# The sixth expert's rows gathered in quarters of 128 columns and turned by VectorE

## The chip, the core and the metric

The kernel runs on one core of one Trainium2 chip. The metric is the device time of one execution, in microseconds (us); the median of three runs of the kernel before is 612.68 us (611.35 to 615.02). The core has TensorE (PE, with its weight loads as PEld), VectorE (DVE), ScalarE (ACT), GpSimd (POOL) and SyncE (SP), each with its own queue of instructions that it takes in order, and 16 DMA engines that move data between the chip's main memory and the on-chip buffer. The matmuls' sums go to a third memory, PSUM.

## The reference

A retention layer of 8 batches, 8 heads, 576 positions and 64 columns makes 4608 rows of 512 numbers, and a mixture of 8 experts works on these rows:

```python
def _moe_ref(x, w_gate, w1, w2):
    N, D = x.shape                       # 4608, 512
    E = w_gate.shape[1]                  # 8
    cap = N // E                         # 576
    flat = (x @ w_gate).flatten()
    order = np.argsort(-flat)
    ...                                  # best pairs first: a token goes to one expert, 576 tokens each
    for e in range(E):
        mask = assigned == e
        h = np.maximum(x[mask] @ w1[e], 0.0)   # 576 x 512 by 512 x 1024
        out[mask] = h @ w2[e]                  # 576 x 1024 by 1024 x 512
```

## The kernel before, in words

The retention layer and the first part of the routing fill the first 160 us. The rows x are then in main memory as `xd`, and also seen as `xq`, in which each row is four quarters of 128 columns. The experts follow one after the other, in an order that the router finds while they run. Experts are counted from 0 here, so the sixth expert is expert 5.

For an expert, `l1` (L1081) computes the first layer in 16 blocks: 8 pieces of 128 hidden columns, each for rows 0 to 255 and for rows 256 to 575. A block is 12 matmuls: four pieces of the 512 columns times three products, since every number is split into a high and a low part (`xh`, `xl`; `w1h`, `w1l`). `l2` (L1132) computes the second layer in five tiles: four of 128 rows, each in 8 steps of three matmuls with 512 columns, and one of 64 rows in 8 short steps of two.

Between these stand the things that the change touches:

- `gather` (L1016) brings the 576 rows of the next expert with POOL's indirect DMAs. For an expert under `PIECES` these are five DMAs of up to 128 whole rows. For the others they are 18 DMAs of 128 rows and 128 columns each, issued one by one as the planner's clock passes 1300 ns for each; their indices are made by `listing` (L505 to L510).
- `transposes` (L1046) puts the rows' columns on the partitions. For an expert under `PIECES` TensorE does it: 20 transposes in five groups of four into PSUM (`pt`, L1074), from which ScalarE copies `xh` and VectorE subtracts to make `xl`. For the others VectorE does it in blocks of 32 by 32 (`xz`, two buffers, L1058), ScalarE copies (L1060) and VectorE subtracts (L1061), and the columns come out in another order, which the second layout of the first-layer weights (`in_w1n`) has too.
- `conv` (L987) splits the weights. Where it is ScalarE and an accumulating POOL load that make the low part, the load is issued by L1009; for experts 6 and 7 it is VectorE (L1002).
- `l2` starts `transposes` of the next expert when the planner's clock `mix.t` is past `state['arrives']`, which `gather` has set 6000 or 9000 ns after its last DMA, and then takes one of its five parts with each step of the second layer.
- The router for the expert after the next runs at the same time. It is a chain: VectorE makes a table `G` (L191), TensorE counts with nine small matmuls (`r`, L383), and VectorE works out the next digit from the counts (L387 to L378). Seven of these chains make a search, followed by the members and the list of the expert (L451, L489). The `Mixer` decides after which matmuls a part of it is put down: it keeps two estimated clocks, `mix.t` for TensorE and `mix.v` for VectorE, and `mix.vec(ns)` adds to the second what a piece of VectorE's work should take.

So the order on each engine is fixed when the program is built, by these estimates, and at run time an engine takes its own queue in order. The lines on which the steps of the change rest are these:

```python
if e + 1 in XG and e + 1 not in XH and mix.t > state['arrives']:
    tr = transposes(e + 1)
next(tr, None)
...
if i == 0 and e >= PIECES:
    for _ in tr:
        pass
```

The second piece, in `l1`, puts down whatever part of the turning is left ahead of the first block.

Of the kernel before, what the change touches and what calls it, by code (L numbers as in the profile page):

```python
# [19 lines left out]
NP, HP, NB = 4, 4, 9  # L20
N, DM, E, FF = 4608, 512, 8, 1024
SLACK = 1.0
PIECES = 6

def consts_np():
    h = np.arange(H); g = (1.0 - 2.0 ** (-5.0 - h)).astype(np.float64)
# [61 lines left out]
class Route:  # L88
# [369 lines left out]
    def listing(s, p):  # L458
# [43 lines left out]
        if early:  # L502
            s.room(cn)
        if p >= PIECES:
            s.quarter = pool.tile([128, 20], I32, name="quarter", bufs=2)  # L505
# [439 lines left out]
def moe(tc, nc, P, R, xd, w1_d, w2_d, out, mix):  # L945
# [12 lines left out]
    def phases():  # L958
        for p in range(E):
# [9 lines left out]
            found.append(R.idx)  # L969
            if p >= PIECES:  # L970
                quarters[p] = R.quarter
# [5 lines left out]
    def dma_pump():  # L977

        while state['dma'] < min(state['conv'] + 4, 8*E):
            e, k = divmod(state['dma'], 8)  # L980
            if e not in regs or state['dma'] >= state['most']:
                return
            t = P['raw']()
            src = ((w1_d[0] if e < PIECES else w1_d[1]) if k < 4 else w2_d)
            nc.sync.dma_start(t, src[bass.ds(regs[e], 1), :, (k % 4)*1024:(k % 4)*1024+1024].rearrange("a p x -> (a p) x"))
            RAW[e, k] = t
            state['dma'] += 1  # L987

    def conv(fast=False):

        e, k = divmod(state['conv'], 8)
        if state['dma'] <= state['conv']:
            mix.drain(lambda: e in regs)
            dma_pump()
        raw = RAW.pop((e, k))
        nm = "w1" if k < 4 else "w2"
        hi = P['w'].tile([128, 1024], F32R, name=nm + "h", bufs=4)
        lo = P['w'].tile([128, 1024], F32R, name=nm + "l", bufs=4)
        A.activation(hi, raw, AF.Copy)
        if e >= PIECES:  # L1000
            for x in (slice(0, 512), slice(512, 1024)):
                V.tensor_tensor(lo[:, x], raw[:, x], hi[:, x].bitcast(F32), op=ALU.subtract)  # L1002
                mix.vec(690)
        elif fast:
            for x in (slice(0, 512), slice(512, 1024)):
                lows.append(lambda x=x: V.tensor_tensor(lo[:, x], raw[:, x], hi[:, x].bitcast(F32), op=ALU.subtract))
        else:
            A.activation(lo, raw, AF.Copy, scale=-1.0)  # L1008
            add = lambda: nc.gpsimd.dma_start(lo, raw, accum_op=ALU.add)  # L1009
            if ready(0) and 0 not in XG:  # L1010
                lows.append(add)
            else:
                add()
        (W1 if k < 4 else W2)[e, k % 4] = (hi, lo)
        state['conv'] += 1
        dma_pump()  # L1016

    def gather(e, all=False):
        if e in XG or not ready(e):
            return  # L1020
        if e >= PIECES:
            if e not in parts:
# [24 lines left out]
    def transposes(e):  # L1047
# [4 lines left out]
        XH[e], XL[e] = xh, xl  # L1052
        if e >= PIECES:
            low = []
# [26 lines left out]
    def l1(e, tr):  # L1081
# [5 lines left out]
        for i, (f, s) in enumerate(order):  # L1087
# [36 lines left out]
            if i in ((2, 4, 7, 10) if e else (5, 7, 9, 11, 13)):  # L1124
                conv()
# [10 lines left out]
    def l2(e, hb):  # L1136
# [43 lines left out]
        for _ in range(want):  # L1180
            conv()
# [115 lines left out]
```

## Time and profile before

| | us |
|---|---|
| median of 3 runs | 612.68 |
| the profiled execution | 614.13 |
| its span, first to last instruction | 612.3 |
| TensorE busy | 593.9 |
| VectorE busy | 421.8 |
| ScalarE busy | 253.7 |
| POOL busy | 246.7 |

The span is cut by stages: the retention layer and the first routing up to about 160 us, then eight times a first and a second layer. Expert 4's second layer begins at 419.18 us and ends at 448.85, expert 5's first layer follows up to 475.69 and its second up to 502.14, and expert 6's first layer follows that. A matmul's end is modelled in this profile, so neighbouring matmuls overlap in it, and the distance between two starts is the better measure of what one takes. A row by stages gives the length, then busy time and instructions of PE, PEld, DVE, ACT and POOL, then the granted clock (1.00 is full speed), the busy share of the DMA engines and what they moved in GB/s. A row of waits gives the total, the number and the longest. In the lines, a name such as `xl<-xz,xh` says which tile is written from which.

### The profile page before, as it was taken

To read this page: it belongs to the slowest core of one execution; us is meant where nothing else is said; L and a number is where in the kernel's file an instruction comes from. 1 tells how busy PE (TensorE), PEld (TensorE's weight loads), DVE (VectorE), ACT (ScalarE), POOL (GpSimd) and SP (SyncE) were. 2 spreads that over 40 slices of the span, in tenths; PEclk is the share of its full clock that TensorE was granted. 3 is DMA by queue.
4 is the path that set the end of the run, shared out by engine and by line. 5 is a ranking of instruction groups with operands and counts; after the bars stand their busy time and mean duration, and the time that the engine had idled before them with its cause. 6 is when DMAs were issued, how large, how long until landed. Compare 5 with 4: busy or idle time off the path is not lost.

```text
span 612.3 us, 14908 instructions
## 1 busy us (share of the span) xinstructions
PE 593.9 (97%) x5778; PEld 515.2 (84%) x5778; DVE 421.8 (69%) x1510; ACT 253.7 (41%) x446; POOL 246.7 (40%) x313
## 2 busy tenths in 40 slices
PE   8999999898999999999999999999999999999994
PEld 5888888775698889879977997898789889989983
DVE  5647696778889788878875886688488755544400
ACT  2334333343554555544461555166245334423310
POOL 5878555505411451352332143233314758711021
PEclk9999999999999999999999999999999999999998
DMA  9999999846885798794986599488928744420010
GB/s 320 408 385 401 296 374 352 262 112 211 211 244 114 248 235 196 248 230 142 246 236 181 109 260 230 116 187 242 251 78 201 198 145 141 149 89 27 2 43 34
DMA packets 49449, 124.84 MB, mean 204 GB/s; under 512 B 7010, under 2 KB 19810, under 8 KB 49378
## 3 DMA queue, kind: packets, MB, share of 16 engines
q1 hardware_dynamic: 36130, 80.10, 37.4%
q0 software_dynamic: 13104, 43.53, 31.2%
q8 instruction: 45, 0.74, 0.5%
q10 hardware_dynamic: 144, 0.26, 0.1%
q14 instruction: 26, 0.21, 0.1%
HBM read 80.35 MB, written 18.87 MB: 162 GB/s over the span
## 4 chain that ended last, share of the span: by engine, by line
PE 72%; issue 12%; DMA 10%; POOL 2%; DVE 1%; SPq 1%; ACT 1%; POOLq 0%; ACTq 0%; DVEq 0%
PE ph L1110 29%; PE py L1153 26%; DMA vin<-in_vk 5%; DMA nin<-in_vk 4%; PE sc L634 3%; PE px L678 3%; PE pS L655 2%; PE r L383 2%; PE pt L1074 2%; PE px L669 2%; POOL out_y L1130 1%; PE pT L710 1%; DMA kin<-in_qk 1%; PE r L489 1%; DMA raw<-in_w 1%
## 5 line engine op out<-in xcount | busy, mean ns | idle before, releaser
L1153 PE MATMUL py<-w2h,hb 128*128 128x512 f32 x576 | 187.3, 397 | 0.0
L1110 PE MATMUL ph<-xh,w1h 128*128 128x320 f32 (+1 forms) x512 | 151.9, 301 | 0.2 <-ACT xh L1076 0.2
L1110 PE MATMUL ph<-xl,w1h 128*128 128x320 f32 (+1 forms) x512 | 149.2, 296 | 0.0
L1110 PE MATMUL ph<-xh,w1l 128*128 128x320 f32 (+1 forms) x512 | 149.0, 296 | 0.0
L1153 PE MATMUL py<-w2l,hb 128*128 128x512 f32 (+1 forms) x320 | 125.2, 391 | 0.0
L1153 PEld LDWEIGHTS py<-w2h,hb 128*128 128x128 f32 x576 | 104.5, 188 | 21.7
L1114 ACT ACTIVATE hb<-ph 128x256 fp32r<-128x256 f32 (+1 forms) x128 | 52.2, 409 | 109.4 <-PE ph L1110 98.2
L1110 PEld LDWEIGHTS ph<-xh,w1h 128*128 128x128 f32 x512 | 96.0, 189 | 1.3 <-ACT xh L1076 0.7
L1110 PEld LDWEIGHTS ph<-xl,w1h 128*128 128x128 f32 x512 | 96.2, 190 | 0.3
L1110 PEld LDWEIGHTS ph<-xh,w1l 128*128 128x128 f32 x512 | 96.0, 189 | 0.0
L1130 POOL DMA_INDIRECT out_y<-yt,idx x40 | 40.3, 1008 | 127.2 <-ACT yt L1173 65.8
L1119 DVE SCALAR_TENSOR_TENSOR hb<-ph,hb 128x256 fp32r<-128x256 f32 (+1 forms) x192 | 57.9, 351 | 27.5 <-ACT hb L1114 26.1
L1153 PEld LDWEIGHTS py<-w2l,hb 128*128 128x128 f32 (+1 forms) x320 | 56.7, 177 | 13.0
L619 POOL TENSOR_TENSOR qin<-qin,cst 128x512 f32<-128x512 f32 (+1 forms) x48 | 47.7, 1022 | 42.6 <-DMA qin<-in_qk 38.5
L1173 ACT ACTIVATE yt<-py 128x512 f32<-128x512 f32 x31 | 18.6, 599 | 92.4 <-PE py L1153 61.5
L658 ACT ACTIVATE st<-pS,cst 128x128 f32<-128x128 f32 x64 | 23.6, 368 | 79.1 <-PE pS L655 79.1
L1009 POOL DMA_DIRECT2D w2l<-raw x24 | 21.7, 906 | 73.3 <-ACT w2l L1008 36.8
L646 DVE TENSOR_TENSOR am<-sc,cst 128x1024 f32<-128x1024 f32 x32 | 39.0, 1218 | 16.5 <-PE sc L634 16.4
L1042 POOL DMA_INDIRECT xg<-xd,idx x30 | 30.2, 1006 | 42.7 <-DVE room L524 16.1
L1030 POOL DMA_INDIRECT xg<-xd,quarter x36 | 37.9, 1054 | 11.1 <-issue 8.7
L634 PE MATMUL sc<-qin,kin 64*128 64x128 f32 x512 | 37.2, 284 | 1.8 <-DMA xd<-raw 1.0
L1009 POOL DMA_DIRECT2D w1l<-raw x23 | 21.2, 937 | 42.4 <-ACT w1l L1008 34.0
(213 smaller groups left out, 932.9 us busy)
## 6 DMA issues: line engine op xcount, KB each, us to landing
raw<-in_w SPq DMA_DIRECT2D x56, 512.0 KB
w2l<-raw POOLq DMA_DIRECT2D x24, 512.0 KB
w1l<-raw POOLq DMA_DIRECT2D x23, 512.0 KB
qin<-in_qk SPq DMA_DIRECT2D x14, 576.0 KB
kin<-in_qk SPq DMA_DIRECT2D x14, 576.0 KB
vin<-in_vk SPq DMA_DIRECT2D x14, 576.0 KB
nin<-in_vk SPq DMA_DIRECT2D x14, 512.0 KB
xd<-raw SPq DMA_DIRECT2D x36, 128.0 KB
```

Of the source, the lines that this page charges most:

```text
L619: nc.gpsimd.tensor_tensor(x, x, e[:, None, :n].to_broadcast([128, (b-a)//n, n]), op=ALU.mult)
L634: nc.tensor.matmul(t[:, h, 128*j:128*j+128], blk(k, 4*g+j)[r], blk(q, 4*g+j)[r], start=(j == 0), stop=True, skip_group_check=True)
L646: nc.vector.tensor_tensor(a, SC[u, g].rearrange("p h (j q) -> p h j q", q=128), m1[:, u % HP, :, None, :].to_broadcast([128, 2, 4, 128]), ...
L658: nc.scalar.activation(s, p, AF.Copy, scale=ss[:, u % HP, c:c+1])
L1009: add = lambda: nc.gpsimd.dma_start(lo, raw, accum_op=ALU.add)
L1030: nc.gpsimd.indirect_dma_start(out=t[:, k, :], out_offset=None, in_=xq[:, :], in_offset=bass.IndirectOffsetOnAxis(ap=quarters[e][:, v:v+1] ...
L1042: nc.gpsimd.indirect_dma_start(out=xg[:n, j, :], out_offset=None, in_=xd[:, :], in_offset=bass.IndirectOffsetOnAxis(ap=found[e][:n, j:j+1] ...
L1110: T.matmul(ps, w, x, start=(k == 0), stop=(k == 11))
L1114: A.activation(hb[:, f, c], ps, AF.Relu)
L1119: V.scalar_tensor_tensor(hb[:, f, to+a:to+b], ps[:, a:b], 0.0, hb[:, f, 256*s+a:256*s+b].bitcast(F32), op0=ALU.max, op1=ALU.subtract)
L1130: st = nc.gpsimd.indirect_dma_start(out=out[:, :], out_offset=bass.IndirectOffsetOnAxis(ap=found[e][:n, t:t+1], axis=0), in_=y[:n], in_off ...
L1153: T.matmul(ps[:m], a, w, start=(k == 0), stop=(k == last), skip_group_check=True)
```

## The change

Two numbers take the place of one. `PIECES`, which chose between whole rows and quarters, between TensorE and VectorE for the turning, and between the two weight layouts, is now 5, and the new `BYDVE`, which chooses who makes the low part of the weights, keeps the 6. So expert 5 is gathered in quarters, turned by VectorE and multiplied with the second layout, while its weights are still split by ScalarE and the accumulating loads.

```diff
-PIECES = 6
+PIECES = 5
+BYDVE = 6
...
         A.activation(hi, raw, AF.Copy)
-        if e >= PIECES:
+        if e >= BYDVE:
             for x in (slice(0, 512), slice(512, 1024)):
```

The added line moves all line numbers behind it by one: L1058 before is L1059 now.

TensorE's five groups of transposes between the first steps of expert 4's second layer are gone from its order. The router's six counting groups in that layer (of 40 steps) stood behind steps 1, 8, 18, 25, 31 and 37 and stand behind steps 1, 8, 15, 22, 28 and 34 now; the seventh stands in expert 5's first layer, in its third block (before: in its second). That layer's list is now behind its eleventh block (before: in its ninth).

VectorE, in the second layer of expert 4, before: one chain of the router ends with the table `G` and the digit `u`, then come the subtractions of expert 5's rows from PSUM (`pt`), and the next chain begins with `cs`.

```order
L191 TENSOR_TENSOR G<-ct,v 128x1152
L378 TENSOR_TENSOR u<-v,D 128x36
L1077 TENSOR_TENSOR xl<-pt,xh 128x4x128 x4
L1077 TENSOR_TENSOR xl<-pt,xh 128x4x64
L387 SCALAR_TENSOR_TENSOR cs<-room,r 32x8
L389 TENSOR_TENSOR cs<-cs,r 32x8 x2
L391 TENSOR_TENSOR f<-r,cs 32x8 x4
```

VectorE at the end of the second layer of expert 4, now, from the third of five subtractions on: `cs` to `G` is the router's sixth chain, `xz` is the last transpose, of 64 rows.

```order
L1062 TENSOR_TENSOR xl<-xz,xh 128x4x128
L388 SCALAR_TENSOR_TENSOR cs<-room,r 32x8
L390 TENSOR_TENSOR cs<-cs,r 32x8 x2
L392 TENSOR_TENSOR f<-r,cs 32x8 x4
L398 TENSOR_REDUCE mq<-f 128x1
L399 STREAM_TRANSPOSE tc<-mq 128x32
L400 TENSOR_REDUCE j<-tc 128x1
L368 TENSOR_SCALAR v<-u,j 128x72
L192 TENSOR_TENSOR G<-ct,v 128x36x16
L1059 STREAM_TRANSPOSE xz<-xg 128x4x64
L1062 TENSOR_TENSOR xl<-xz,xh 128x4x128
L1062 TENSOR_TENSOR xl<-xz,xh 128x4x64
```

What was one piece of five subtractions is now five transposes and five subtractions, they stand three chains later in the program, and the sixth chain stands between the third subtraction and the last transpose.

ScalarE at the end of the second layer of expert 5, before: `yt` is the output copy of a tile of the second layer, `xh` the copies of expert 6's turned rows, `hb` the first block of expert 6's first layer.

```order
L999 ACTIVATE w1h<-raw 128x1024
L1173 ACTIVATE yt<-py 128x512
L1060 ACTIVATE xh<-xz 128x4x128 x4
L1173 ACTIVATE yt<-py 128x512
L1060 ACTIVATE xh<-xz 128x4x64
L1175 ACTIVATE yt<-py 64x512
L1114 ACTIVATE hb<-ph 128x256
```

The same place now:

```order
L1000 ACTIVATE w1h<-raw 128x1024
L1174 ACTIVATE yt<-py 128x512 x2
L1061 ACTIVATE xh<-xz 128x4x128 x4
L1061 ACTIVATE xh<-xz 128x4x64
L1176 ACTIVATE yt<-py 64x512
L1115 ACTIVATE hb<-ph 128x256
```

The output copy of the fourth tile moved ahead of the four copies of expert 6's rows, and the fifth follows them directly.

## Rows read from the trace of the kernel before

**Rows 1.** The page: busy time of TensorE, share of the span, instructions.

```profile
PE 593.9 (97%) x5778; PEld 515.2 (84%) x5778; DVE 421.8 (69%) x1510; ACT 253.7 (41%) x446; POOL 246.7 (40%) x313
```

**Rows 2.** Expert 4's second layer: busy time (instructions) of each engine, granted clock, DMA.

```profile
419.18:448.85 29.67, 29.67 (x189) 23.06 (x188) 18.41 (x81) 12.96 (x18) 7.92 (x13) 1.00 0.79 198
```

**Rows 3.** Timeline of TensorE, expert 4's second layer: start, length, line, operation.

```profile
420.12 0.51 PE L1074 MATMUL pt<-ident,xg 128*128 128x128 f32 x4
...
425.75 0.62 PE L1153 MATMUL py<-w2h,hb 128*128 128x512 f32 x2
...
426.44 0.62 PE L1153 MATMUL py<-w2h,hb 128*128 128x512 f32 x2
...
427.14 0.39 PE L383 MATMUL r<-oh,G 128*128 128x32 bf16 x9
...
428.15 0.62 PE L1153 MATMUL py<-w2h,hb 128*128 128x512 f32 x2
```

**Rows 4.** One chain of the router in that layer: TensorE's group, then VectorE's first and last.

```profile
443.81 0.39 PE L383 MATMUL r<-oh,G 128*128 128x32 bf16 x9
...
444.23 0.15 DVE L387 SCALAR_TENSOR_TENSOR cs<-room,r 32x8 f32<-32x8 f32 x1 [1.58 <-PE r L383]
...
446.86 0.19 DVE L378 TENSOR_TENSOR u<-v,D 128x36 f32<-128x36 bf16 x1
```

**Rows 5.** Expert 6's rows turned: timeline of VectorE, then of ScalarE.

```profile
490.60 1.30 DVE L1058 STREAM_TRANSPOSE xz<-xg 128x512 f32<-128x512 f32 x2
494.85 0.69 DVE L1061 TENSOR_TENSOR xl<-xz,xh 128x512 fp32r<-128x512 f32 x1 [2.96 <-issue]
...
497.54 0.65 DVE L1061 TENSOR_TENSOR xl<-xz,xh 128x512 fp32r<-128x512 f32 x1
498.24 0.45 DVE L1058 STREAM_TRANSPOSE xz<-xg 128x256 f32<-128x256 f32 x1
498.61 0.65 DVE L1061 TENSOR_TENSOR xl<-xz,xh 128x512 fp32r<-128x512 f32 x1
500.53 0.43 DVE L1061 TENSOR_TENSOR xl<-xz,xh 128x256 fp32r<-128x256 f32 x1 [1.27 <-ACT xh L1060]
...
493.70 0.60 ACT L1173 ACTIVATE yt<-py 128x512 f32<-128x512 f32 x1 [4.34 <-PE py L1153]
494.20 1.14 ACT L1060 ACTIVATE xh<-xz 128x512 fp32r<-128x512 f32 x2
...
499.59 0.60 ACT L1173 ACTIVATE yt<-py 128x512 f32<-128x512 f32 x1 [1.31 <-PE py L1153]
```

**Rows 6.** Timeline of TensorE: expert 5's last tile, expert 6's first and second block.

```profile
498.44 0.39 PE L1153 MATMUL py<-w2h,hb 128*128 128x512 f32 x1
...
502.14 0.28 PE L1110 MATMUL ph<-xh,w1h 128*128 128x256 f32 x1
...
503.72 0.31 PE L1110 MATMUL ph<-xl,w1h 128*128 128x320 f32 x1
```

**Rows 7.** Quarter indices on VectorE, and first and last gather of 18 on POOL.

```profile
466.18 0.17 DVE L506 TENSOR_SCALAR lo<-lo 32x40 f32<-32x40 f32 x1
...
467.54 0.17 DVE L510 TENSOR_SCALAR quarter<-quarter 32x20 int32<-32x20 int32 x1
...
467.99 1.07 POOL L1030 DMA_INDIRECT xg<-xd,quarter  x1 [2.19 <-DVE eb L534]
...
495.62 0.96 POOL L1030 DMA_INDIRECT xg<-xd,quarter  x1 [0.30 <-issue]
```

**Rows 8.** Clock at the end, TensorE's first and last matmuls, its longest waits.

```profile
606.50:607.00 0.50, 0.00 (x0) 0.00 (x0) 0.00 (x0) 0.00 (x0) 0.09 (x1) 0.94 0.00 0
...
1.47 5.08 PE L1248 MATMUL warm<-full 128*128 128x512 bf16 x12 [1.47 <-DVE full L1234]
...
604.04 0.39 PE L1153 MATMUL py<-w2l,hb 128*128 128x512 f32 x1
...
PE pS L655 <- DMA vin<-in_vk: 3.9, 3, 2.0
```

## The prediction

> **What bounds the kernel now.** I read the page first, then the stages with their granted clock, then the timelines of TensorE, VectorE and ScalarE around the change. The page has TensorE busy for 593.9 us of 612.3 [rows 1]. In the stage that the change enters, the second layer of the fifth expert (expert 4, counted from 0), TensorE is busy for all of 29.67 us at the full clock, while VectorE is busy for 18.41 [rows 2]. So an edit gains only what it takes out of TensorE's own row, and loses whatever makes TensorE wait. From here on I use the clock of the profiled execution.
>
> **What the change removes.** The 20 transposes of the sixth expert (expert 5) leave TensorE. They stand in five groups between the steps of that second layer. From the first group to the first undisturbed step it is 425.75 - 420.12 = 5.63 us, with five steps in it. An undisturbed step takes 426.44 - 425.75 = 0.69, so the turning costs 5.63 - 5 x 0.69 = 2.18 us [rows 3]. The stage as a whole gives another figure. It has 32 such steps, 8 short ones for the last 64 rows (3.70 us together, from 498.44 to 502.14 in the next expert [rows 6]) and 6 counting groups of the router. One of those adds 428.15 - 427.14 - 0.69 = 0.32 [rows 3]. Without turning that is 32 x 0.69 + 3.70 + 6 x 0.32 = 27.70, and 29.67 - 27.70 = 1.97. I take 2.1, with 1.9 to 2.2 as its bounds. Five copies and five subtractions from PSUM go too; they are replaced one for one.
>
> **What it adds off TensorE.** Seven small VectorE operations make the quarter indices; between the start of the first and of the last before they cost 467.54 - 466.18 = 1.36 us [rows 7], some 1.5 with the last one. They push the router's chain back by that much, which is hidden as long as the chain has its table ready for TensorE's next group; if it were not, the whole 1.5 us would be a wait of TensorE in front of the first group; the sum holds it at nothing, since VectorE stands idle for 11 of the stage's 29.67 us [rows 2]. POOL issues 18 small gathers where it issued 5. For expert 6 the first and the last of 18 start 467.99 and 495.62 [rows 7], with one accumulating load and two scatters among them. That is 27.6 us for 20 steps, 1.38 each. For expert 5 the last is the 25th in POOL's order (18 quarters, with five accumulating loads and two scatters among them), so 24 x 1.38 = 33 us after the first. I estimate the first at 412.5, from its place in the order: the list that it reads stands behind the ninth of sixteen blocks of the layer that ends at 419.18. That makes 445.6 for the last. The rows that it brings are turned at 450.3 (below), so this is hidden, with some 4 us for the flight. SyncE's queue loads the same bytes in the same order, from the second layout. The accumulating loads among the quarters come later by the quarters ahead of them. The last of these loads is 24th, near 444, and the last fourth of the following layer is the first to read it, some twenty microseconds on.
>
> **The wait that comes: the first layer of expert 5.** TensorE now needs ten results of VectorE and ScalarE for expert 5, and the order shows where they stand. Five transposes, in two buffers, alternate with five subtractions, each of which waits for ScalarE's copy. Ahead of the first stands the router's fifth chain, and between the third subtraction and the last transpose stands the sixth. Engines take their queues in order, so these chains are paid too.
> When does the fifth chain start? TensorE's fifth counting group now stands behind 28 steps and 4 groups: 419.18 + 28 x 0.69 + 4 x 0.32 = 439.78. A chain starts 444.23 - 443.81 = 0.42 after its group and takes 446.86 - 444.23 = 2.63 up to its last small operation of 0.19 [rows 4]. So the first transpose starts at 439.78 + 0.42 + 2.63 + 0.19 = 443.02. Two transposes take 1.30, and the first subtraction starts at 444.32. From first to third subtraction it is 497.54 - 494.85 = 2.69, and 0.70 more to the next operation [rows 5]: 447.71. The sixth chain holds VectorE until 450.34. Then come the short last transpose (0.37 until the next start), 0.65 for the fourth subtraction and 0.43 for the fifth [rows 5]: it ends at 451.79.
> TensorE starts that layer at 419.18 + 27.70 = 446.88. Its first block needs only the first two subtractions, which are ready. Its second block reads the last one 503.72 - 502.14 = 1.58 after the layer's start [rows 6], at 448.46. It waits 451.79 - 448.46 = 3.3 us. Both times move with the same steps, so the difference is firmer than either. Below, the ten operations back to back without a handshake take 6.0 us and give 3.2; above, five handshakes 0.1 longer each give 3.8. I take 3.4.
>
> **The second wait: the first layer of expert 6.** The added work moves the planner's clock, and expert 6 now begins to be turned one tile of 128 rows later. On ScalarE all five of its copies stand behind the output copy of the fourth tile, where four stood ahead of it. That copy started at 499.59, 1.15 after the last tile's first matmul (498.44), and a copy of the turning follows an output copy after 0.50 (493.70 to 494.20) [rows 5, 6]. From the first copy to the end of the fifth subtraction: 0.65 to the first subtraction, 3.39 to the last transpose (498.24 - 494.85), 0.37, 0.65 and 0.43: 5.49 [rows 5]. So the end is at 499.59 + 0.50 + 5.49 = 505.58, and TensorE wants it at 503.72 [rows 6]: 1.9 us. The output copy cannot start before the tile's last matmul ends, about 498.6, which would make it 0.9. I take 1.5. Before the change the same result came at 500.96, ahead of the layer. Expert 7 is turned in the old order.
>
> **The sum.** 2.1 gained, 3.4 and 1.5 lost: 2.8 us longer. The profiled execution took 614.13 us (its span 612.3), so it becomes 616.9. It lies 1.45 above the median of the runs, 612.68, so I forecast a median of 615.5. The bounds of the terms (-2.2 + 3.2 + 0.9 and -1.9 + 3.8 + 1.9) make it 1.9 to 3.8 us longer: 614.6 to 616.5.
>
> **Rivals.**
> *The clock falls in the wait.* TensorE stands idle for 3.4 us. In this trace the granted clock is 0.94 in the mean of the half microsecond up to 607.0: of its two levels, 2.4 GHz for 0.44 us and 1.2 for the rest, so it fell at 606.94, some 2.5 us after the last matmul ended at 604.43, and the longest wait inside the work is 2.0 us, with no fall [rows 8]. So this wait is longer than the one idle time that was seen to end in half speed and than all that were not. The price: the twelve matmuls of 512 columns at the start took 5.08 us, 0.42 each, the 1.2 GHz level; the three of a step take 0.69, 0.23 each, the level of 2.4 [rows 3, 8]. Half speed for as long as that start costs 2.5 us: 618.0. Against it: one fall is all there is to see, and it need not come at the same point of every idle time. Chance 0.35.
> The Trainium skill ("TensorE: Matmul & The Clock Gate", section "HAM oscillation — how this bites in real kernels") says that a wait in which TensorE falls idle can send its clock back to half, to be earned again. By that rule the sum is 618.0, by the longest wait in the trace it stays 615.5; the fall at the end sides with the rule, and no row here shows a wait of this length inside the work.
> *No wait comes, so it is not slower.* The wait is inferred from the order. If TensorE's second block were released by the first subtractions alone, or the router's sixth chain were overtaken, both waits would be nothing and 2.1 us would be left: 610.6. For it: that idle time of VectorE. Against it: the idle time lies before the fifth chain, and a queue in order cannot use it. Chance 0.07.
> *The gather is the bound.* Quarters share a queue with four accumulating loads of 512 KB. If the last of them landed at 454 instead of 447 or so, the last transpose would start 3.7 later, 619.2. It decides from 450.3 on. Against it: expert 6's last quarter was issued at 495.62 and its rows turned at 498.24 without a wait. Chance 0.08.
> That the change does not do what it says is out: the order shows the transposes on VectorE.
>
> **How the numbers follow.** The forecast has 0.50, the rivals 0.35, 0.07 and 0.08. 0.5% is 3.1 us, about what a measurement of this kernel can tell from no change: 609.6 to 615.7. The forecast lies just inside, so some 0.20 of its 0.50 is slower; with the clock (0.33 of 0.35) and the gather (all but 0.02) that is about 0.57 slower. The no-wait case is inside too, and only a better gain than any row shows would be faster: 0.03. The rest, 0.40, is the same. The range leaves out the no-wait case and the far end of the others: 613.2 to 619.0; the forecast's own is 614.6 to 616.5.
>
> **What would show it.** No transposes on TensorE in expert 4's second layer, which takes some 27.7 us. Then TensorE idle for about 3.4 us behind the first block of expert 5's first layer, released by VectorE's subtraction, with the router's chain right ahead of the last transpose; and idle for 1 to 2 us at the same place of expert 6. A granted clock under 1.00 in the first of these stretches would give the clock its part. I am wrong if TensorE's row is closed there, if it waits for a DMA, or if the time is under 613.

## The result and the profile after

The kernel after the change takes 618.73 us in the median of 15 runs (617.16 to 624.32), the kernel before on the same chip 614.16 (611.35 to 619.88): a ratio of 1.0082, 95% interval 1.0065 to 1.0099. The forecast was 615.5, with 614.6 to 616.5 as its own range and 613.2 to 619.0 with the rivals; the time lies above the first and inside the second, near the price of the clock's rival, 618.0. Against the kernel before it is 4.57 us longer, where 2.8 were forecast. Three later sets, on three chips, gave the kernel after the change more: 630.16, 624.89 and 625.79 us, ratios 1.0226 [1.0195, 1.0257], 1.0146 [1.0092, 1.0200] and 1.0169 [1.0117, 1.0221], while the kernel before stayed at 615.1 to 615.3. So there are two things to explain.

The profiled execution of after took 624.32 us, its slowest run, with a span of 622.5: 10.2 us more than before's. TensorE's starts divide that. The first expert starts 5.85 us later (167.88 against 162.03), in the part that the change does not touch. There the granted clock fell to half for a while, which it did not in before:

```profile
125.66:132.49 6.83, 5.77 (x66) 5.33 (x68) 2.68 (x5) 1.33 (x3) 2.18 (x3) 0.50 0.54 145
```

Eight of the eighteen profiles have such a fall ahead of the first expert and start it at 162.98 to 167.88 us; the ten without start it at 160.34 to 162.72. Among the eight is e11, the kernel before with an edit that comes much later, so this part is not the change's. From there to TensorE's last matmul it is 3.25 us longer, and 1.1 more lie behind that (the last matmul starts 8.3 us ahead of the end before and 9.4 after). The stages show where the 3.25 are:

| stage, start to start, us | before | after | e9 | e13 | e5 |
|---|---|---|---|---|---|
| expert 4, second layer | 29.67 | 27.47 | 29.76 | 31.32 | 32.06 |
| expert 5, first layer | 26.84 | 31.60 | 32.04 | 30.26 | 31.94 |
| expert 5, second layer | 26.45 | 26.39 | 29.94 | 28.26 | 32.20 |
| expert 6, first layer | 25.59 | 26.58 | 26.08 | 26.58 | 26.46 |

(e5, e9 and e13 are the same kernel in the later sets, told of below. The other stages together are 0.24 us shorter in after.) First the page of after and the windows of these stages, with half a microsecond at three places of expert 5's first layer; they answer to [rows 1, 2].

```profile
PE 596.9 (96%) x5758; PEld 517.8 (83%) x5758; DVE 425.9 (68%) x1523; ACT 254.7 (41%) x446; POOL 260.0 (42%) x326
```

```profile
424.79:452.26 27.47, 27.47 (x168) 21.46 (x167) 19.69 (x86) 12.06 (x16) 21.67 (x25) 1.00 0.82 197
452.26:483.86 31.60, 28.75 (x214) 28.21 (x213) 24.45 (x100) 15.11 (x27) 8.58 (x10) 0.95 0.64 165
483.86:510.25 26.39, 26.39 (x125) 21.10 (x124) 17.82 (x57) 8.29 (x12) 20.30 (x25) 1.00 0.62 186
510.25:536.83 26.58, 26.11 (x193) 25.67 (x192) 15.09 (x36) 11.58 (x22) 20.29 (x33) 1.00 0.40 127
456.50:457.00 0.50, 0.31 (x1) 0.26 (x1) 0.50 (x2) 0.48 (x2) 0.00 (x0) 0.75 0.00 0
458.50:459.00 0.50, 0.50 (x4) 0.50 (x3) 0.00 (x0) 0.00 (x0) 0.50 (x1) 0.50 0.00 0
460.50:461.00 0.50, 0.50 (x8) 0.45 (x8) 0.12 (x1) 0.35 (x1) 0.00 (x0) 1.00 0.00 0
```

TensorE is 2.20 us shorter where its turning went, and still full there. In the next stage it is idle for 31.60 - 28.75 = 2.85 us, and just as the idle time ends the granted clock goes to 0.50, which is 1.2 GHz. TensorE's timeline at that place, where expert 5's first layer starts (answering to [rows 6]):

```profile
452.26 0.28 PE L1111 MATMUL ph<-xh,w1h 128*128 128x256 f32 x1
...
453.56 0.28 PE L1111 MATMUL ph<-xh,w1l 128*128 128x256 f32 x1
456.69 0.61 PE L1111 MATMUL ph<-xh,w1h 128*128 128x320 f32 x1 [2.85 <-ACT xh L1061]
457.15 0.63 PE L1111 MATMUL ph<-xl,w1h 128*128 128x320 f32 x1
...
460.22 0.28 PE L1111 MATMUL ph<-xh,w1h 128*128 128x256 f32 x1
```

The first block runs through, the second waits. Its matmul that reads `xl` starts 457.15 - 452.26 = 4.89 us into the layer, where 1.58 was undisturbed [rows 6]. The second block then takes 460.22 - 456.69 = 3.53 us, twice what it takes at the full clock. VectorE's timeline says what it waited for (answering to [rows 4, 5]):

```profile
448.25 0.19 DVE L379 TENSOR_TENSOR u<-v,D 128x36 f32<-128x36 bf16 x1
448.36 1.30 DVE L1059 STREAM_TRANSPOSE xz<-xg 128x512 f32<-128x512 f32 x2
...
452.44 0.65 DVE L1062 TENSOR_TENSOR xl<-xz,xh 128x512 fp32r<-128x512 f32 x1
453.12 0.15 DVE L388 SCALAR_TENSOR_TENSOR cs<-room,r 32x8 f32<-32x8 f32 x1
...
455.37 0.46 DVE L192 TENSOR_TENSOR G<-ct,v 128x576 bf16<-128x576 bf16 x1
455.75 0.44 DVE L1059 STREAM_TRANSPOSE xz<-xg 128x256 f32<-128x256 f32 x1
456.11 0.98 DVE L1062 TENSOR_TENSOR xl<-xz,xh 128x512 fp32r<-128x512 f32 x2
```

No row has an idle time in brackets: VectorE goes from the fifth chain into the turning, from the third subtraction into the sixth chain, from that into the last transpose, and the last subtraction ends at 457.09, right ahead of the matmul at 457.15. The queue's order is the wait, but another was right behind it: the last of the 18 quarters was issued at 448.84 and took 6.7 us to land, so the transpose at 455.75 could not have started before 455.5. At expert 6 a queue's order is seen in small, ScalarE first, then TensorE:

```profile
506.80 0.60 ACT L1174 ACTIVATE yt<-py 128x512 f32<-128x512 f32 x1 [4.89 <-PE py L1154]
507.29 1.14 ACT L1061 ACTIVATE xh<-xz 128x512 fp32r<-128x512 f32 x2
```

```profile
512.26 0.41 PE L1111 MATMUL ph<-xh,w1h 128*128 128x320 f32 x1 [0.43 <-ACT xh L1061]
```

All copies of the turning stand behind the fourth tile's output copy.

The 1.1 us behind the last matmul are in POOL's closing drain, an instruction with which the program ends. Before, then after (number, then shortest, median and longest in ns):

```profile
L1291 POOLq DRAIN  x3: 46/107/6136, 605.4 to 612.1; - x3
L1292 POOLq DRAIN  x3: 46/107/7238, 614.5 to 622.3; - x3
```

It goes with the number of DMAs that POOL has issued. From TensorE's last matmul to the end it is 8.30 us in both profiles with 154 of them (before, e8), 8.42 with 155 (e10, e15), 9.36 in the kernel before with 13 more (e11, e16), and 9.40 in all eleven profiles that gather as after does, with 167.

### The profile page after: what moved, and what is told of

The parts are those of the page before. It is cut to its first block, busy times and chain, and to the rows that moved or that the text cites. A ratio compares the mean times of both kernels' runs of the same rounds, so it can differ in the third digit from the quotient of the medians.

```text
span 622.5 us, 14893 instructions
## 1 busy us (share of the span) xinstructions
PE 596.9 (96%) x5758; PEld 517.8 (83%) x5758; DVE 425.9 (68%) x1523; ACT 254.7 (41%) x446; POOL 260.0 (42%) x326
## 4 chain that ended last, share of the span: by engine, by line
PE 67%; issue 13%; DMA 9%; POOL 4%; DVE 3%; ACT 1%; SPq 1%; POOLq 0%; ACTq 0%; DVEq 0%
PE ph L1111 28%; PE py L1154 21%; PE sc L635 3%; PE px L679 3%; DMA vin<-in_vk 3%; DMA qin<-in_qk 2%; PE pS L656 2%; PE px L670 2%; POOL out_y L1131 2%; PE r L384 2%; PE pt L1075 1%; PE pT L711 1%; DMA nin<-in_vk 1%; POOL xg L1031 1%; DMA xg<-xd,quarter 1%
## 5 line engine op out<-in xcount | busy, mean ns | idle before, releaser
L1120 DVE SCALAR_TENSOR_TENSOR hb<-ph,hb 128x256 fp32r<-128x256 f32 (+1 forms) x192 | 57.7, 350 | 28.5 <-ACT hb L1115 27.3
L1031 POOL DMA_INDIRECT xg<-xd,quarter x54 | 55.8, 1033 | 22.6 <-issue 11.6
L635 PE MATMUL sc<-qin,kin 64*128 64x128 f32 x512 | 38.5, 289 | 3.7 <-POOL qin L620 2.3
L1043 POOL DMA_INDIRECT xg<-xd,idx x25 | 25.2, 1009 | 39.8 <-DVE room L525 14.4
L635 PEld LDWEIGHTS sc<-qin,kin 64*128 64x128 f32 x512 | 32.2, 191 | 8.6 <-POOL qin L620 3.7
```

The source lines that it names most:

```text
L635: nc.tensor.matmul(t[:, h, 128*j:128*j+128], blk(k, 4*g+j)[r], blk(q, 4*g+j)[r], start=(j == 0), stop=True, skip_group_check=True)
L1031: nc.gpsimd.indirect_dma_start(out=t[:, k, :], out_offset=None, in_=xq[:, :], in_offset=bass.IndirectOffsetOnAxis(ap=quarters[e][:, v:v+1] ...
L1043: nc.gpsimd.indirect_dma_start(out=xg[:n, j, :], out_offset=None, in_=xd[:, :], in_offset=bass.IndirectOffsetOnAxis(ap=found[e][:n, j:j+1] ...
L1120: V.scalar_tensor_tensor(hb[:, f, to+a:to+b], ps[:, a:b], 0.0, hb[:, f, 256*s+a:256*s+b].bitcast(F32), op0=ALU.max, op1=ALU.subtract)
```

## The experiments

Each set has its own runs of the kernel before: 614.02 us in the first (e1 to e4), 615.34 in the second (e5 to e8), 615.15 in the third (e9 to e12), 615.09 in the fourth (e13 to e16). Stages are read as in the table above. The first set has no run of the unchanged kernel after the change, so e1 to e4 are compared by their stages.

**e1_chain_behind: the router's chain behind the turning.** The Mixer puts no part of the router down while expert 5 is being turned, so the sixth chain comes after the turning.

```diff
...
-                mix.adv(650)
+                mix.adv(650, state.get('turning') == e + 1)
```

> The router's sixth chain of VectorE is put behind the turning of expert 5's rows; nothing else is moved. Theory (the chain in front of the last transpose makes the wait of 2.85 us, and the wait lets the clock fall): the last transpose can start when its quarters have landed, about 453.0 (last issue 448.84 and a median flight of 4.2), the fifth subtraction ends near 454.9, TensorE wants it at 453.9: a wait of about 1 us and no fall. Expert 5's first layer takes 28.0 us instead of 31.6, the time is about 3.6 us below that of the changed kernel, some 615.1. Rival (the last quarters land late and the chain only fills the gap): the wait stays 2.5 us or more, the layer 30 us or more, the time within 1 us of 618.7.

623.15 us, ratio 1.0132 [1.0102, 1.0162]. The wait at the second block fell from 2.85 to 1.73 us, the clock stayed at 1.00 there, and the layer took 29.15 instead of 31.60:

```profile
451.97 0.41 PE L1113 MATMUL ph<-xh,w1h 128*128 128x320 f32 x1 [1.73 <-ACT xh L1062]
...
507.00 0.39 PE L1113 MATMUL ph<-xh,w1h 128*128 128x256 f32 x1 [2.59 <-ACT xh L1062]
508.53 0.53 PE L1113 MATMUL ph<-xl,w1h 128*128 128x256 f32 x1 [1.14 <-DVE xl L1063]
```

So the chain was in the wait, for 1.12 us of it. What is left is the gather: VectorE now waits for the last quarters.

```profile
451.02 0.45 DVE L1060 STREAM_TRANSPOSE xz<-xg 128x256 f32<-128x256 f32 x1 [1.53 <-DMA xg<-xd,quarter]
```

And the chain held back sends everything behind it later: expert 6's rows are late by 2.59 and 1.14, its first layer takes 28.69, and the time is not the 615.1 of the theory.

**e2_warm_in_wait: TensorE kept busy in the wait.** Twelve matmuls of the kind at the program's start stand between the first and the second block.

```diff
+            if e == 5 and i == 1:
+                P['warm'](12)
```

> The changed kernel with twelve matmuls of 512 columns on a constant tile between the first and the second block of expert 5's first layer, where TensorE waits; the wait itself stays. Theory (of the 4.76 us that this layer lost, 1.77 are the half clock): the granted clock stays 1.00, the block behind the wait takes 1.76 us instead of 3.53, the layer 29.8 us, the time is some 1.8 us lower, 617.0. Rival (the clock has no part in the time, or falls for another reason than the idle time): the layer stays at 31.5 and the time at 618.7.

623.90 us, 1.0139 [1.0116, 1.0161]. The clock stayed at 1.00 in that layer, which took 30.24; the next run shows that it can do so without these matmuls, so this does not tell that they held it. Expert 4's second layer took 31.58, with a wait of 2.5 us for the router's table `G`, which neither theory had, and the clock fell there. Expert 6's rows were late by 2.67 and 1.14 us.

**e3_six_early: expert 6 turned one tile earlier again.**

```diff
-                state['arrives'] = mix.t + 6000
+                state['arrives'] = mix.t + (6000 if e != 6 else 1600)
```

> Expert 6's rows begin to be turned about one tile of 128 rows earlier in the program, as before the change; expert 5 is left as changed. Theory (the order of ScalarE's copies behind the fourth tile's output copy makes the second wait): expert 6's first layer takes 25.6 us instead of 26.6, the time is 1.0 lower, 617.7. Rival (its last quarter, which is now issued 2.2 us later against the layer than before, would be waited for anyway): the layer stays at 26.3 to 26.6. The first wait of 2.85 us and its fall of the clock stay in both.

624.42 us, 1.0162 [1.0137, 1.0187]. Expert 6's first layer is back at 25.58, without a wait: that term is its place behind the output copy. It also gave an unplanned answer on the clock. TensorE's wait in expert 5's first layer, then that stage and half a microsecond of it in the wait and after it:

```profile
458.46 0.41 PE L1111 MATMUL ph<-xh,w1h 128*128 128x320 f32 x1 [2.85 <-ACT xh L1061]
```

```profile
454.03:484.28 30.25, 27.36 (x215) 26.79 (x214) 24.46 (x100) 15.11 (x27) 8.59 (x10) 1.00 0.61 146
458.00:458.50 0.50, 0.04 (x1) 0.04 (x1) 0.50 (x2) 0.48 (x2) 0.00 (x0) 1.00 0.00 0
459.50:460.00 0.50, 0.50 (x5) 0.50 (x5) 0.50 (x2) 0.00 (x0) 0.00 (x0) 1.00 0.00 0
```

The same 2.85 us, and no fall. The layer takes 30.25, 3.41 more than before the change: this is the wait's price alone, and 31.60 - 30.25 = 1.35 that of the fall.

**e4_gated_and_six: each tile turned when its quarters are due.** As e3, and expert 5's parts follow the planner's clock one by one.

```diff
...
+                    if turned < 5 and mix.t > state.get((5, (3, 7, 11, 15, 17)[turned]), 1e9) + (8000 if turned < 4 else 6000):
+                        next(tr)
...
```

> Each tile of expert 5 is turned as soon as its own quarters should have landed, so that three of the five stand ahead of the router's fifth chain and the last ahead of the sixth; expert 6 begins one tile earlier too. Theory (both waits are the order's, and nothing else was lost): expert 4's second layer 27.5 us, expert 5's first 26.8 to 27.3, expert 6's first 25.6, no fall of the clock; against the kernel before only the 2.2 us gained are left, and some 0.4 lost to the last quarters: 612.4. Rival (VectorE now waits for quarters in front of the router's chains, and these come too late for TensorE): expert 4's second layer grows by 1 to 3 us, time 614 to 616.

625.20 us, 1.0178 [1.0156, 1.0200]. Only the last transpose still had to wait for its quarters, and it stood ahead of the sixth chain:

```profile
448.67 0.45 DVE L1061 STREAM_TRANSPOSE xz<-xg 128x256 f32<-128x256 f32 x1 [4.20 <-DMA xg<-xd,quarter]
```

So the chain came late: TensorE waited 4.5 us for `G` in expert 5's first layer, which took 33.08: the wait that the rival had, though not its time of 614 to 616. What VectorE's queue gives to one it takes from the other.

**e5_after_again, e9_after_third, e13_after_base: no edit.**

> The changed kernel once more, word for word, as a base for the others on the same chip. The four kernels tried so far were all 623 to 625, also the two that only fill or shift the wait, and their traces show TensorE waiting for the router's tables in expert 4's second layer (1.1 to 2.5 us), which the first trace of the changed kernel does not show. Theory A (these waits belong to the changed kernel as well and come and go from run to run): the changed kernel is again 618 to 624 here, with such a wait in this trace. Theory B (they come from the edits tried): it is 618.7 again with no such wait.

> The changed kernel a third time, as the base of this set. Its first trace had no late signal of TensorE and 618.7; its second had the router's first steps on VectorE start 2.3 and 3.9 us after TensorE's counting groups in expert 4's second layer, TensorE waiting 2.7 us there for the next table, a crawl of TensorE of 5 us in expert 5's second layer, and 630. Theory (the lateness comes with POOL's gathers and differs from chip to chip): the lateness is there or not as a whole, and the time goes with it, 618 to 630. Rival (it was a single disturbed set): 618.7 again.

> The changed kernel as the base of this set. Two sets out of three had TensorE's signals late and 625 to 630 us, one did not and had 618.7. Both theories of the other runs need the base only to know which of the two this set is.

630.16, 624.89 and 625.79 us; the stages stand in the table above. Expert 5's first layer behaves as in the first profile, with the fall in e5 and e9 (waits of 3.08 and 3.19 us) and without it in e13 (2.85). New are the second layers of experts 4 and 5. Of e13, VectorE and then TensorE in expert 4's second layer (`r` is TensorE's counting group, `cs` the first operation of the chain that reads it; "remote" is a release that the profile puts down to no instruction):

```profile
424.16 0.15 DVE L388 SCALAR_TENSOR_TENSOR cs<-room,r 32x8 f32<-32x8 f32 x1 [0.18 <-issue]
426.64 0.76 DVE L192 TENSOR_TENSOR G<-ct,v 128x1152 bf16<-128x1152 bf16 x1
...
431.40 0.15 DVE L388 SCALAR_TENSOR_TENSOR cs<-room,r 32x8 f32<-32x8 f32 x1 [3.89 <-remote]
433.93 0.76 DVE L192 TENSOR_TENSOR G<-ct,v 128x1152 bf16<-128x1152 bf16 x1
```

```profile
427.46 0.39 PE L384 MATMUL r<-oh,G 128*128 128x32 bf16 x9
...
434.74 0.39 PE L384 MATMUL r<-oh,G 128*128 128x32 bf16 x9 [2.03 <-DVE G L192]
```

The group at 427.46 is read at 431.40, 3.94 us later, while VectorE stands idle until it is released: the signal is late, not VectorE. In e5 and e9 the same distance is 4.28 and 3.30. In the first profile of after the same distance was 0.43 (a group at 430.59, `cs` at 431.02). Then TensorE waits 2.03 us for the table, and the clock falls behind this wait:

```profile
435.40:435.90 0.50, 0.50 (x3) 0.37 (x2) 0.43 (x3) 0.00 (x0) 0.20 (x2) 0.67 1.11 221
435.90:436.40 0.50, 0.50 (x3) 0.40 (x2) 0.46 (x4) 0.21 (x1) 0.50 (x1) 0.50 1.02 205
```

In expert 5's second layer of e5 TensorE itself goes slowly, with idle times that no semaphore explains ("issue"):

```profile
505.35 0.40 PE L1154 MATMUL py<-w2h,hb 128*128 128x512 f32 x1 [0.30 <-issue]
...
508.18 0.49 PE L1154 MATMUL py<-w2h,hb 128*128 128x512 f32 x1 [1.03 <-issue]
```

Why this can cost anything now is in the two first profiles. VectorE's first two chains in expert 4's second layer, before, and then after:

```profile
420.32 0.14 DVE L387 SCALAR_TENSOR_TENSOR cs<-room,r 32x8 f32<-32x8 f32 x1
422.67 0.76 DVE L191 TENSOR_TENSOR G<-ct,v 128x1152 bf16<-128x1152 bf16 x1
427.57 0.15 DVE L387 SCALAR_TENSOR_TENSOR cs<-room,r 32x8 f32<-32x8 f32 x1 [1.19 <-PE r L383]
```

```profile
427.04 0.14 DVE L388 SCALAR_TENSOR_TENSOR cs<-room,r 32x8 f32<-32x8 f32 x1
429.31 0.76 DVE L192 TENSOR_TENSOR G<-ct,v 128x1152 bf16<-128x1152 bf16 x1
431.02 0.15 DVE L388 SCALAR_TENSOR_TENSOR cs<-room,r 32x8 f32<-32x8 f32 x1 [0.85 <-PE r L384]
```

Before, the table was ready at 423.43 and TensorE's next group stood at 427.14 [rows 3]: 3.7 us to spare. After, it is ready at 430.07 for the group at 430.59: 0.5 to spare. The turning on TensorE stood between these groups, 2.2 us of the 3.2 lost. The other 1.1 is VectorE's: it starts the first chain 1.55 us after its group (425.49), without an idle time, where it was 0.44 before (419.88).

**e6_cover_both, e7_cover_part, e8_before_cover: work put into the wait.** The first layer begins with blocks that need only the first two tiles of rows: four in e6 (and two for expert 6), two in e7. e8 is the kernel before with e6's edit.

```diff
         if e == 0:
             order[:8] = [(f, s) for s in range(2) for f in range(4)]
+        if e == 5:
+            order[:4] = [(f, s) for s in range(2) for f in range(2)]
```

(e7; e6 has all eight for expert 5, and these four for expert 6, and gives one block's sums another PSUM buffer.)

> The changed kernel with TensorE's order of blocks altered: in expert 5's first layer the four blocks of the first 256 columns of four feature groups come first, in expert 6's two of them, so that the block that needs the last subtraction starts 4.3 and 1.4 us later and has work ahead of it. No other engine's queue is touched. Theory (both waits are only a matter of what stands ahead of that block, and the fall of the clock comes from the first): expert 5's first layer 26.9 us instead of 31.6, expert 6's 25.6 instead of 26.6, the time 5.7 us below the changed kernel run beside it. Rival (the end of VectorE's chain sets the layer's end anyway, since the two following operations on each block stand behind it): the layers shrink by less than half of that.

> The changed kernel with two blocks instead of one ahead of the waiting one in expert 5's first layer only; expert 6 stays as changed. TensorE has 1.42 us more of work, so of the wait of 2.85 some 1.4 is left. Theory (the wait's length decides on the clock): no half speed there, the layer takes 28.3 us, the time is 1.4 + 1.8 = 3.2 us below the changed kernel beside it. Rival (any wait there lets the clock fall): the layer takes 30.1 us and the time is 1.4 lower.

> The kernel before with the same altered order of blocks in experts 5 and 6, as a control of that edit. It has no wait at either place, so there is nothing to cover. Theory (the order of blocks costs nothing by itself): 614.1, within 0.3%. Rival (the order itself gains or loses, by when ScalarE and VectorE get their blocks): more than 0.5% off, and the run with both covered has to be read against this one.

e7 took 625.76 us, 1.0171 [1.0146, 1.0197], the unchanged kernel beside it 630.16. Its wait was 1.41 us and its layer 28.82, without a fall:

```profile
457.29 0.41 PE L1113 MATMUL ph<-xh,w1h 128*128 128x320 f32 x1 [1.41 <-ACT xh L1061]
```

e6 took 628.59, 1.0226 [1.0203, 1.0249]. More cover did not help: TensorE waits longer, now for VectorE to empty a block's sums, though without a fall of the clock, and the layer takes 30.56.

```profile
460.66 0.41 PE L1113 MATMUL ph<-xh,w1h 128*128 128x320 f32 x1 [3.48 <-DVE hb L1122]
```

That operation stands in VectorE's queue behind the turning and the chain, so VectorE's end sets the layer. Expert 6's first layer grew to 29.81, with its rows late by 2.87 and 1.14 us. e8 took 615.77, 1.0021 [1.0000, 1.0041]: the order by itself costs little in time, but 0.93 us in expert 5's first layer (27.77 against 26.84), which belongs to e6's 30.56.

**e10_whole_rows, e15_rows_for_all: fewer gathers.** Expert 5 still turned by VectorE, its rows by four gathers of 128 whole rows and two of quarters; the two labels are one kernel in two sets. The columns of these rows then lie otherwise than the second weight layout has them: the kernel leaves out the matching of the two, so expert 5's output is not the layer's, and only its time is read.

```diff
+                if e == 5 and k < 16:
+                    if k % 4 == 3:
+                        nc.gpsimd.indirect_dma_start(out=t[:, k-3:k+1, :]..., in_=xd[:, :], ...)
```

> The changed kernel with expert 5's rows brought by four gathers of whole rows and two of quarters in place of 18 of quarters: the same bytes, a third of the gathers. The turning is unchanged and so works on rows in another layout: the output of expert 5 is not the reference's. Theory G (the number of POOL's gathers in expert 4's second layer makes TensorE's signals late there): no late start of the router's steps, that layer 27.5 us and not 30 to 32; the crawl in expert 5's second layer stays, since expert 6 keeps its 18 quarters. Rival (something else in the layer, such as the accumulating loads or the missing transposes): the lateness stays, the layer is again 30 us or more. Where the set shows no lateness in the base, both say 27.5.

> Expert 5's rows again by four whole-row gathers and two of quarters (its output is then not the reference's), as a repeat on this chip beside its base. Theory G: expert 4's second layer 27.5 us without a late start of the router, 3 us or so below the base; the layer after next keeps its crawl. Rival (the first such run lay on a good chip): no difference to the base.

622.34 and 621.43 us, 1.0103 [1.0070, 1.0137] and 1.0091 [1.0055, 1.0128], where the unchanged kernel beside them took 624.89 and 625.79. Of the difference, 1.0 us is the shorter drain at the end (8.42 against 9.40). Expert 4's second layer took 27.47 and 27.48: the late signals are gone. VectorE of e15, whose groups start at 425.73 and 430.83:

```profile
426.16 0.15 DVE L388 SCALAR_TENSOR_TENSOR cs<-room,r 32x8 f32<-32x8 f32 x1 [1.11 <-PE r L384]
...
431.25 0.15 DVE L388 SCALAR_TENSOR_TENSOR cs<-room,r 32x8 f32<-32x8 f32 x1 [1.96 <-PE r L384]
```

Both are read after 0.43 us. The lateness stayed where expert 6's 18 quarters are gathered, in expert 5's second layer (31.30 and 29.91). The wait of 2.85 us is in both; the clock fell behind it in e10 (31.70) and not in e15 (30.25).

**e11_before_gathers, e16_before_dense: more gathers in the kernel before.** Thirteen further gathers of a quarter in expert 4's second layer, in e11 into two slots in turn, so that they waited for each other, in e16 into 13 slots.

```diff
+                if e == 4 and state.get('extra', 99) < 13 and mix.t >= state.get('extra_at', 0):
+                    nc.gpsimd.indirect_dma_start(out=state['scratch'][:, x], ..., in_=xq[:, :], ...)
```

> The kernel before with 13 gathers of 128 quarters into a scratch tile put among POOL's work of expert 4's second layer; nobody reads what they bring. Theory G: TensorE's signals come late in that layer here too. Since its counting groups stand 7.2 us apart in the first two tiles, up to 3 us of lateness is taken up there and the layer grows by less than 1 us; from the third on they stand 5.1 apart, so a wait of 1 to 2 us is possible there. Time 614 to 617. Rival (gathers cost TensorE nothing): no late start, the layer 29.7 and the time as before, within 0.3%.

> The kernel before with 13 gathers of 128 quarters in expert 4's second layer as tried, but each into a place of its own, so that none waits for another to land and they follow each other as closely as the changed kernel's. Nobody reads them. Theory G: the router's first steps start 2 us or more late in that layer, also without the change; TensorE's groups are further apart there, so the layer grows by 0 to 2 us, the time is 614 to 617. Rival (the lateness needs something else of the change): no late start.

615.85 us, 1.0011 [0.9978, 1.0043], and 617.32, 1.0038 [1.0009, 1.0067]. The stage took 29.93 and 29.75, and the first five chains started on time in both, at most 0.5 us later behind their groups than before. e16's sixth did not; its group stands at 445.38:

```profile
447.04 0.15 DVE L387 SCALAR_TENSOR_TENSOR cs<-room,r 32x8 f32<-32x8 f32 x1 [1.60 <-PE py L1155]
```

That is 1.66 us after the group instead of 0.43; TensorE then waited 0.69 us for the table, and expert 5's first layer took 27.70 against 26.84. So these gathers did not make the lateness of the changed kernel, 3.3 to 4.3 us at the second chain. Whether they made this smaller one a single profile does not show. e11's gathers were too sparse to tell.

**e12_loads_by_vector: the accumulating loads taken away.** Four of expert 5's first-layer weight parts are split by VectorE.

```diff
-        if e >= BYDVE:
+        if e >= BYDVE or e == 5 and k < 4:
```

> The changed kernel with the low parts of expert 5's first-layer weights made by VectorE (eight subtractions, 10.4 us in two layers) instead of POOL's four accumulating loads, which stand among the 18 quarters. By the order the sixth chain now stands behind the last subtraction. Theory: POOL ends its quarters some 5 us earlier, the rows are turned earlier, the wait of 2.9 us in expert 5's first layer falls to under 1; if the loads make the signals late, this goes too and the time is 8 to 12 us below the base of this set. Theory G: the lateness in expert 4's second layer stays, and VectorE's added work makes its tables later still; only the first wait is gained, 3 to 5 us below the base.

624.65 us, 1.0117 [1.0060, 1.0174]. The lateness stayed (expert 4's second layer 32.97), so these loads are not needed for it. The waits in expert 5's first layer fell to 0.64 and 0.67 us (29.00), but VectorE's added work cost expert 6 5.0 us of waits.

**e14_router_apart: wider spaces between the router's groups.** In expert 4's second layer the Mixer leaves more time for a chain, in the next layer less.

```diff
+        if e == 4:
+            mix.slack = 2.4
...
+        if e == 5:
+            mix.slack = 1.0
```

> The changed kernel with the planner's pace of the router's steps changed: in expert 4's second layer its counting groups stand 11 to 12 steps of TensorE apart (7.5 to 8 us) instead of 7 (5.1), in expert 5's first layer as close as they can. The 18 quarters stay. Theory G (late signals cost time only through the next table): VectorE's first steps again start 2 to 5 us late, but TensorE does not wait for a table, and expert 4's second layer takes 27.3 to 27.6 us; the sixth chain no longer stands in front of the last transpose, so expert 5's first layer takes 27 to 28.5. Expert 6 is found some 6 us later and pays for it, 3 to 6 us in its first layer. Rival (TensorE itself is slowed): the layer stays at 29.5 us or more.

637.79 us, 1.0350 [1.0286, 1.0413]. The stage took 26.81, without any wait, though the first chains of the stage still started late: groups at 418.63 and 427.14, and

```profile
421.18 0.15 DVE L388 SCALAR_TENSOR_TENSOR cs<-room,r 32x8 f32<-32x8 f32 x1 [0.93 <-remote]
...
428.59 0.15 DVE L388 SCALAR_TENSOR_TENSOR cs<-room,r 32x8 f32<-32x8 f32 x1 [4.12 <-PE r L384]
```

2.55 and 1.45 us after their groups. So in this stage lateness cost only through the table that TensorE wants next. The chains pushed out of this stage are paid in the next two, 36.75 and 39.21 us long, where e13's were 30.26 and 28.26; the expectation had 27 to 28.5 for the first of them.

## Why the prediction was right and wrong

*What goes* was right: 2.20 us forecast as 2.1, bounds 1.9 to 2.2.

*The wait in expert 5's first layer* was right in place and size. The chain of queues came as written: fifth chain, turning, sixth chain, last transpose, last subtraction. The matmul that needs it was late by 4.89 - 1.58 = 3.31 us, and without a fall the layer is 3.41 longer (e3, e13, e15), against 3.4. The row's 2.85 is less, since it ends at the matmul before, which needs `xh` alone. e1 showed that the chain is part of it, e6 that VectorE's end sets it. It also showed what the forecast did not have: without the chain the gather takes its place, after 1.12 of the 2.85 us.

*The second wait* was 0.99 us, with 1.5 taken and 0.9 as a bound; e3 showed its cause. *The gather* was ready, but by luck. The last quarter was issued 24.05 us into expert 4's second layer (448.84), 2.4 earlier than I had it (445.6, or 26.4 into it). It then took 6.7 us to land where I had left some 4, and was there 0.2 us ahead of the last transpose, which followed the chain without a gap. So that rival did not come true in the profile of after, and it did in e1 and e4, where the chain was out of the way. The rival without a wait is out.

*The first step that failed* is the choice of the clock's level: the forecast held the wait at the full clock, the rival with 0.35 did not. In the profile of after the fall came at the forecast place. Its price was overrated: 1.35 us in that stage instead of 2.5.

*The second* is a term that the sum held at nothing: "POOL issues 18 small gathers where it issued 5" was judged by whether they are hidden behind TensorE. Their 13 more DMAs cost 1.10 us where nothing hides them, in the closing drain. The terms as measured make -2.20 + 3.41 + 0.99 + 1.35 + 1.10 = 4.65 us, and the medians differ by 4.57. That this is so close is partly luck, since the terms come from single profiles and the clock differs from run to run: time x (1 - clock) is 5.62 us in the mean of after's 15 runs, 4.3 in the run with the median time, 8.1 in the profiled one, and 3.2 to 3.8 in the mean of before's runs in the four later sets. What of it lies behind TensorE's last matmul costs nothing.

What decides the fall is not settled by the idle time's length. In expert 5's first layer, 2.85 us ended in half speed in after and e10, not in e3, e13 and e15; 3.48 us did not in e6, 1.41 and 1.73 did not in e7 and e1. In expert 4's second layer 1.91 us did in e3 and 2.03 in e13, 2.04 and 2.08 did not in e6 and e7. The Trainium skill ("TensorE: Matmul & The Clock Gate", section "HAM oscillation — how this bites in real kernels") tells of a kernel in which a wait for a DMA sends the clock back to half each time round. The waits here could do it, and e3, e6, e13 and e15 show that they need not.

*The third step that failed*, which the later sets show, is "hidden as long as the chain has its table ready", held at nothing since VectorE stood idle for 11 us of the stage. I had added the seven index operations to that chain and not looked at its margin: the turning had been 2.2 us of cover between the router's groups, and its going, with 1.1 us of later start on VectorE, left 0.5 us of 3.7. In the later sets VectorE is released 3.3 to 4.3 us after the group, and the stage gives back all that it had gained (29.76 to 32.06 against 27.47). That this goes through the table is shown by TensorE's waits for it and by e14. With whole rows in place of expert 5's small gathers it was gone in both sets (e10, e15). As many gathers in the kernel before did not bring it (e16, but for the one chain at the stage's end), and it does not need the accumulating loads (e12).

Three things stay open: what else makes the signals late; why the first profile has none of it; and why TensorE goes slowly beside expert 6's quarters in expert 5's second layer, where the kernel before has the same 18 without it. Counting 16 records of landing to a transfer, the traces with the lateness lack 881 to 1217 of some 6000 to 6192, and the first profile of after lacks 26 of 6192. But traces of the kernel before lack 865 and 977 of 5984 too and are fast; whether the recording has a part in it was not tried.

## What to carry to other kernels

Work on the bounding engine is also the cover of every chain that another engine runs between two of its steps: before it is taken away, read from the trace by how much each such result is early, not how long the other engine stands idle. Where a wait of some microseconds is new on TensorE, give it two prices, with the clock and without. Ask of a term that is hidden behind the bounding engine whether it is also hidden after that engine's last instruction. And take the unchanged kernel along in each set: here the change cost 0.8% in the first set and 1.5 to 2.3% in three others.

## What the runs showed of the hardware that was not expected

A wait of 2.85 us behind the same matmul ended at half the clock in two executions (after, e10) and at the full clock in three (e3, e13, e15). A result of TensorE released an idle VectorE 0.43 us after its group began in the first profile of after and 3.30 to 4.28 us after it in three others of the same program (e5, e9, e13), while 18 gathers of 128 columns were under way; with six gathers in their place it was 0.43 again (e10, e15). POOL's closing drain took 6.14 us when POOL had issued 154 DMAs and 7.24 when it had issued 167.
